# Moving the start of the FFN's moving operands from chunk to chunk

## The chip, the cores and the metric

The kernel runs on one core of a Trainium2 chip. The metric is the device time of one execution in microseconds. Before the change two runs took 2716.68 and 2721.58 us, median 2719.13 us.

## The reference

For each of 8 sequences of 3008 tokens and 256 features the reference takes a real FFT along the sequence, applies a complex linear layer (`w_r`, `w_i`, biases), shrinks real and imaginary parts towards zero by 0.01, and transforms back. All 24064 tokens then pass a feed-forward network (FFN) with 2048 hidden features:

```python
X = np.fft.rfft(x, axis=1)                      # per sequence
Yr = Xr @ w_r - Xi @ w_i + b_r; Yi = Xr @ w_i + Xi @ w_r + b_i
Yr, Yi = shrink(Yr, 0.01), shrink(Yi, 0.01)
y = np.fft.irfft(Yr + 1j * Yi, n=3008, axis=1)
h = y @ w_in; g = h - np.tanh(h); out = g @ w_out
```

## The kernel before, in words

The FFT is split into 47 and 64 points, 3008 being 47 times 64. Three parts follow each other per sequence and overlap across sequences.

**Forward** (lines 196 to 250) transforms 47 points at a time: three one-pass matmuls with a moving operand of 94 x 512 (lines 225 to 227), or, for the first sequence, one full fp32 matmul (line 219), which the chip carries out as two records. **Spectrum** does the 64-point step (line 277), the linear layer (line 297, moving operand 128 x 256), the shrinking and the first inverse step (lines 332 to 334).

**Chunk** is the FFN, in 52 chunks. A chunk has 5 pairs of rows of 94 tokens, so n = 470 columns; the last two chunks have 282. `time` makes the last inverse step (line 415) and writes the result as two fp32r parts, `yh` by ScalarE (line 419) and `yl` by VectorE (line 420). Such a pair of parts, high and low, is how the kernel keeps fp32 precision with one-pass matmuls: a product is low times high, high times low, and high times high. For each of 16 blocks `f` of 128 hidden features, `up` runs six matmuls with `yh` and `yl` moving (line 428), then tanh on ScalarE (line 431), `g` on VectorE (line 433), `gh` on ScalarE (line 435) and `gl` on VectorE (line 437). `down` runs six matmuls with `gh` and `gl` moving into two accumulators `o` (line 449). That is 192 FFN matmuls a chunk and 9984 in the kernel. `store` copies `o` out and sends it off.

The order of all work on each engine is fixed by the order in which the program issues it. The last loop issues, for each step `g`, `up` of block `g + 2`, then the Forward, Spectrum and `time` work planned for that step, then `down` of block `g`. Between the last matmul of `up(f)` and the first of `down(f)` stand therefore two `down` and two `up` of neighbouring blocks. The PSUM tile `h` has two buffers, `gh` and `gl` three each, `yh` and `yl` two each.

Where tiles lie: the pool `const` comes first in on-chip memory, and in it the four weight tiles `win_h`, `win_l`, `wout_h`, `wout_l`, whose 512-byte blocks begin at 128 modulo 512 bytes in each partition. Then comes `below`, a tile of 128 + 8 floats of which only the first column is read, then everything else. In the FFN the moving tiles have rows of `PITCH` = 512 floats (2048 bytes), though only 470 are used, so that all buffers of `yh`, `yl`, `gh` and `gl` begin at the same place modulo 512, which is 160. The moving operands of lines 225 to 227, 297 and 332 to 334 begin at 160 too.

Of the kernel before, what the change touches and what calls it, by code (L numbers as in the profile page):

```python
# [10 lines left out]
F32 = mybir.dt.float32  # L11
F32R = mybir.dt.float32r
# [54 lines left out]
def spectral_ffn(ctx, tc, x, w_r, w_i, b_r, b_i, w_in, w_out, f1, f2, i1, i2, out):  # L67
    nc = tc.nc
    P = 128
# [3 lines left out]
    CT = CP * 94  # L73
    NF = FF // P
    PITCH = 512
    PSUM = bass.MemoryType.PSUM

    const = ctx.enter_context(tc.tile_pool(name="const", bufs=1))
    load = ctx.enter_context(tc.tile_pool(name="load", bufs=2))
    work = ctx.enter_context(tc.tile_pool(name="work", bufs=2))  # L80
    cvt = ctx.enter_context(tc.tile_pool(name="cvt", bufs=2))
    ffn = ctx.enter_context(tc.tile_pool(name="ffn", bufs=3))
# [114 lines left out]
    class Forward:  # L197
        def __init__(self, b, ch):
            self.b, self.ch = b, ch
            self.x, self.ps = {}, {}  # L200
# [141 lines left out]
    class WholeSpectrum(Spectrum):  # L342
# [28 lines left out]
        def shrink(self):  # L371
            y = self.add(lambda jj, ri: self.tb[jj * 64:(jj + 1) * 64, :])
            up = self.temp("up", "th")
            nc.scalar.activation(out=up, in_=y, func=AF.Relu, bias=below[:, :1])
            mn = self.mn = work.tile([P, 2, D], F32, name="mn", tag="tmp", bufs=4)
            nc.vector.tensor_scalar(out=mn, in0=y, scalar1=LAM, scalar2=0.0, op0=ALU.add, op1=ALU.min)
            self.up = up
# [15 lines left out]
    class Chunk:  # L393
        def __init__(self, c):
            self.c, self.n = c, sizes[c] * 94
            self.pairs = [(p // NP, p % NP) for p in range(begin[c], begin[c] + sizes[c])]

        def load(self, lo=0, hi=96):
# [9 lines left out]
        def time(self, t):  # L408
            n = self.n
            if t == 0:  # L410
                self.yh = work.tile([P, 2, PITCH], F32R, name="yh", tag="yh")
                self.yl = work.tile([P, 2, PITCH], F32R, name="yl", tag="yl")
            ps = ps_f.tile([P, 512], F32, name="ps_i2", tag="f")
            for k, (_, p) in enumerate(self.pairs):
                nc.tensor.matmul(  # L415
                    ps[:, k * 94:(k + 1) * 94], self.zt[:, k, t * P:(t + 1) * P], i2t[:, p * 94:(p + 1) * 94],
                    start=True, stop=True,
                )
            nc.scalar.copy(out=self.yh[:, t, :n], in_=ps[:, :n])
            nc.vector.tensor_tensor(out=self.yl[:, t, :n], in0=ps[:, :n], in1=self.yh[:, t, :n].bitcast(F32), op=ALU.subtract)  # L420

        def up(self, f):
            n = self.n
            h = ps_h.tile([P, 512], F32, name="h", tag="h")
            k = 0
            for lhs, rhs in ((win_l, self.yh), (win_h, self.yh), (win_h, self.yl)):
                for t in range(2):
                    nc.tensor.matmul(h[:, :n], lhs[:, t, f * P:(f + 1) * P], rhs[:, t, :n], start=k == 0, stop=k == 5)  # L428
                    k += 1
            th = ffn.tile([P, CT], F32, name="th", tag="th")  # L430
            nc.scalar.activation(out=th[:, :n], in_=h[:, :n], func=AF.Tanh)  # L431
            g = ffn.tile([P, CT], F32, name="g", tag="g")
            nc.vector.tensor_tensor(out=g[:, :n], in0=h[:, :n], in1=th[:, :n], op=ALU.subtract)  # L433
            gh = ffn.tile([P, PITCH], F32R, name="gh", tag="g_h")
            nc.scalar.copy(out=gh[:, :n], in_=g[:, :n])  # L435
            gl = ffn.tile([P, PITCH], F32R, name="gl", tag="g_l")
            nc.vector.tensor_tensor(out=gl[:, :n], in0=g[:, :n], in1=gh[:, :n].bitcast(F32), op=ALU.subtract)  # L437
            return gh, gl

# [56 lines left out]
    with tc.manual_schedule(engines={E.PE, E.Activation, E.DVE, E.Pool, E.SP}):  # L496
# [6 lines left out]
        def keep_warm(n):  # L503
            for _ in range(n):
                nc.tensor.matmul(idle, warm[:, :P], warm, start=True, stop=True)

        keep_warm(8)
        below = const.tile([P, P + 8], F32, name="below")
        nc.vector.memset(below, -LAM)
        f1f = load_whole(f1, [P, P], "f1")  # L510
        first = [Forward(0, ch) for ch in range(NP // XC)]
# [128 lines left out]
    for g in range(-AHEAD, len(order)):  # L640
        if g + AHEAD < len(order):
            c, f = order[g + AHEAD]
# [4 lines left out]
        c, f = order[g]  # L647
# [33 lines left out]
```

## Time and profile before

| | |
|---|---|
| median of two runs | 2719.13 us (2716.68 to 2721.58) |
| profiled execution | 2722.2 us; span of its instructions 2720.4 us |
| mean granted TensorE clock | 0.993 |
| busy, TensorE matmul (PE) | 2685.2 us, 99% |
| busy, weight loads (PEld) | 2388.2 us, 88% |
| busy, VectorE (DVE) / ScalarE (ACT) / GpSimd (POOL) | 1741.2 / 1369.4 / 58.1 us |

Times in the views are microseconds, and the last number of a group is the mean of one instruction in nanoseconds. Matmuls are pipelined: a 128 x 470 matmul is on record for about 370 ns, but the next one starts long before it ends. What a matmul costs the kernel is the distance from its start to the next one's start. "Lnnn" is a line of the kernel; `o<-gh,wout_h` reads "writes `o`, reads `gh` and `wout_h`".

### The profile page before, as it was taken

How to read it: one execution, taken by the hardware profiler on the slowest of the kernel's cores; microseconds unless marked ns; L12 is line 12 of the kernel's file. 1: busy time of each engine (PE TensorE's matmuls, PEld its weight loads, DVE VectorE, ACT ScalarE, POOL GpSimd, SP SyncE). 2: the span in 40 equal slices, each digit the busy share in tenths (PEclk: the TensorE clock that was granted, in tenths of full speed). 3: DMA queues.
4: the chain of work that ended last, by engine and by line, in shares of the span. 5: the costliest groups of instructions: out<-in, count | busy, mean ns of one | idle time of the engine just before them, and what ended most of it. 6: DMA issues, size and time to landing. Idle time of an engine off the chain costs nothing.

```text
span 2720.4 us, 36889 instructions
## 1 busy us (share of the span) xinstructions
PE 2685.2 (99%) x14114; PEld 2388.2 (88%) x14114; DVE 1741.2 (64%) x3059; ACT 1369.4 (50%) x2571; POOL 58.1 (2%) x47
## 2 busy tenths in 40 slices
PE   8799999999999999999999999999999999999999
PEld 6578888999889998899988999899988999998989
DVE  5696776666656666566665666657675666655555
ACT  3564455444554445544455454644446444444445
POOL 2140000000000000000000000000000000000000
PEclk8899999999999999999999999999999999999999
DMA  6532114111141113211123110311104111100000
GB/s 207 153 100 66 57 50 127 38 53 36 31 119 45 42 36 92 75 49 41 36 58 101 38 50 29 111 56 49 49 22 123 45 42 40 35 22 22 20 19 17
DMA packets 105217, 163.52 MB, mean 60 GB/s; under 512 B 7440, under 2 KB 71056, under 8 KB 104944
## 3 DMA queue, kind: packets, MB, share of 16 engines
q1 hardware_dynamic: 105040, 161.16, 19.6%
q8 instruction: 111, 1.82, 0.3%
q14 instruction: 66, 0.54, 0.1%
HBM read 86.16 MB, written 74.97 MB: 59 GB/s over the span
## 4 chain that ended last, share of the span: by engine, by line
PE 92%; DVE 5%; ACT 1%; DMA 1%; issue 1%; POOL 0%; SPq 0%; DVEq 0%; ACTq 0%; POOLq 0%
PE o L449 36%; PE h L428 36%; PE ps_v L297 4%; PE ps_i L415 4%; PE ps_f L277 3%; PE ps_t L297 2%; PE ps_f L225 1%; DVE y L322 1%; PE ps_f L226 1%; PE ps_f L227 1%; PE ps_i L333 1%; PE ps_i L334 1%; PE ps_i L332 1%; DVE g L433 1%; DVE gl L437 0%
## 5 line engine op out<-in xcount | busy, mean ns | idle before, releaser
L433 DVE TENSOR_TENSOR g<-h,th 128x470 f32<-128x470 f32 (+1 forms) x832 | 531.5, 639 | 557.0 <-ACT th L431 549.3
L431 ACT ACTIVATE th<-h 128x470 f32<-128x470 f32 (+1 forms) x832 | 463.1, 557 | 769.8 <-PE h L428 769.4
L437 DVE TENSOR_TENSOR gl<-g,gh 128x470 fp32r<-128x470 f32 (+1 forms) x832 | 532.2, 640 | 288.9 <-ACT gh L435 205.0
L435 ACT CAST gh<-g 128x470 fp32r<-128x470 f32 (+1 forms) x832 | 483.0, 581 | 393.5 <-DVE g L433 385.5
L449 PE MATMUL o<-gh,wout_l 128*128 128x470 f32 (+1 forms) x1664 | 633.3, 381 | 0.8 <-ACT gh L435 0.8
L449 PE MATMUL o<-gl,wout_h 128*128 128x470 f32 (+1 forms) x1664 | 616.9, 371 | 2.6 <-DVE gl L437 2.6
L449 PE MATMUL o<-gh,wout_h 128*128 128x470 f32 (+1 forms) x1664 | 616.4, 370 | 0.0
L428 PE MATMUL h<-yh,win_l 128*128 128x470 f32 (+1 forms) x1664 | 482.4, 371 | 5.2 <-DVE g L433 4.7
L428 PE MATMUL h<-yl,win_h 128*128 128x470 f32 (+1 forms) x1664 | 481.2, 370 | 0.0
L428 PE MATMUL h<-yh,win_h 128*128 128x470 f32 (+1 forms) x1664 | 481.2, 370 | 0.0
L449 PEld LDWEIGHTS o<-gl,wout_h 128*128 128x128 f32 x1664 | 313.2, 188 | 44.4 <-DVE gl L437 5.7
L428 PEld LDWEIGHTS h<-yh,win_l 128*128 128x128 f32 x1664 | 310.5, 188 | 44.4 <-DVE g L433 6.6
L449 PEld LDWEIGHTS o<-gh,wout_l 128*128 128x128 f32 x1664 | 313.6, 188 | 36.5 <-issue 1.5
L428 PEld LDWEIGHTS h<-yl,win_h 128*128 128x128 f32 x1664 | 311.3, 188 | 35.7
L428 PEld LDWEIGHTS h<-yh,win_h 128*128 128x128 f32 x1664 | 311.2, 188 | 35.6
L449 PEld LDWEIGHTS o<-gh,wout_h 128*128 128x128 f32 x1664 | 314.0, 189 | 32.2
L322 DVE TENSOR_TENSOR y<-tb,ps_v 64x256 f32<-64x256 f32 x384 | 160.0, 417 | 13.1 <-ACT tb L369 9.1
L415 PEld LDWEIGHTS ps_i<-i,zin 96*128 96x128 f32 x1024 | 128.6, 195 | 5.4 <-issue 2.2
L415 PE MATMUL ps_i<-i,zin 96*128 96x94 f32 x1024 | 130.1, 275 | 1.4 <-DMA zin<-z 1.4
L277 PEld LDWEIGHTS ps_f<-f,at 128*128 128x128 f32 x768 | 101.2, 192 | 14.1 <-issue 9.0
L277 PE MATMUL ps_f<-f,at 128*128 128x128 f32 x768 | 102.8, 276 | 6.5 <-DMA at<-a 6.5
L92 DVE TENSOR_TENSOR x_l<-xt,x_h 94x512 fp32r<-94x512 f32 x112 | 78.6, 708 | 44.8 <-ACT x_h L91 44.8
(99 smaller groups left out, 2103.6 us busy)
## 6 DMA issues: line engine op xcount, KB each, us to landing
xt<-in_x SPq DMA_DIRECT2D x64, 384.0 KB, 3.7
at<-a SPq DMA_DIRECT2D x96, 256.0 KB, 2.8
z<-zo SPq DMA_DIRECT2D x96, 256.0 KB, 2.4
out<-ot SPq DMA_DIRECT2D x50, 470.0 KB, 3.0
a<-st SPq DMA_DIRECT2D x56, 384.0 KB, 3.1
zin<-z SPq DMA_DIRECT2D x42, 480.0 KB, 4.2
w_raw<-in_moe_w_in SPq DMA_DIRECT2D x8, 512.0 KB, 4.3
w_raw<-in_moe_w_out SPq DMA_DIRECT2D x8, 512.0 KB, 3.9
```

The source lines that it names most:

```text
L92: rest.tensor_tensor(out=lo, in0=src, in1=hi.bitcast(F32), op=ALU.subtract)
L225: nc.tensor.matmul(pv, f1h, xl, start=True, stop=False)
L277: nc.tensor.matmul(pv[:, t, jj], self.at[:, jj, t * P:(t + 1) * P], rhs, start=True, stop=True)
L297: nc.tensor.matmul(dst, lhs[:, t], rhs[:, t, :], start=n == 0, stop=n == 5)
L322: nc.vector.tensor_tensor(out=y[ri * 64:(ri + 1) * 64, jj, :], in0=common(jj, ri), in1=self.vv[jj * 64:(jj + 1) * 64, ri * D:(ri + 1) * D] ...
L415: nc.tensor.matmul(ps[:, k * 94:(k + 1) * 94], self.zt[:, k, t * P:(t + 1) * P], i2t[:, p * 94:(p + 1) * 94], start=True, stop=True,)
L428: nc.tensor.matmul(h[:, :n], lhs[:, t, f * P:(f + 1) * P], rhs[:, t, :n], start=k == 0, stop=k == 5)
L431: nc.scalar.activation(out=th[:, :n], in_=h[:, :n], func=AF.Tanh)
L433: nc.vector.tensor_tensor(out=g[:, :n], in0=h[:, :n], in1=th[:, :n], op=ALU.subtract)
L435: nc.scalar.copy(out=gh[:, :n], in_=g[:, :n])
L437: nc.vector.tensor_tensor(out=gl[:, :n], in0=g[:, :n], in1=gh[:, :n].bitcast(F32), op=ALU.subtract)
L449: nc.tensor.matmul(self.o[t][:, :n], lhs[:, f, t * P:(t + 1) * P], rhs[:, :n], start=f == 0 and k == 0, stop=f == NF - 1 and k == 2,)
```

## The change

Each chunk `c` gets a number `at` = 2 * (c % 21) floats, that is 0, 8, ..., 160 bytes, and its `yh`, `yl`, `gh` and `gl` begin that far into their tiles. `below` loses its 8 spare floats, so everything allocated after it lies 32 bytes lower: the tiles begin at 128 modulo 512, and the FFN's moving operands at 128 + 8 * (c % 21). The largest `at` is 40 floats, and 40 + 470 fits in the row of 512. The number, size and order of instructions stay as they were. The same starts are written by ScalarE (`yh`, `gh`) and VectorE (`yl`, `gl`).

```diff
     class Chunk:
         def __init__(self, c):
             self.c, self.n = c, sizes[c] * 94
+            self.at = 2 * (c % 21)
...
-                self.yh = work.tile([P, 2, PITCH], F32R, name="yh", tag="yh")
-                self.yl = work.tile([P, 2, PITCH], F32R, name="yl", tag="yl")
+                self.yh = work.tile([P, 2, PITCH], F32R, name="yh", tag="yh")[:, :, self.at:self.at + CT]
+                self.yl = work.tile([P, 2, PITCH], F32R, name="yl", tag="yl")[:, :, self.at:self.at + CT]
...
-            gh = ffn.tile([P, PITCH], F32R, name="gh", tag="g_h")
+            gh = ffn.tile([P, PITCH], F32R, name="gh", tag="g_h")[:, self.at:]
...
-            gl = ffn.tile([P, PITCH], F32R, name="gl", tag="g_l")
+            gl = ffn.tile([P, PITCH], F32R, name="gl", tag="g_l")[:, self.at:]
...
-        below = const.tile([P, P + 8], F32, name="below")
+        below = const.tile([P, P], F32, name="below")
```

## The prediction

> **What bounds the kernel now.** I read the page first: the busy shares, the granted clock in slices, and the chain of waits that ended last.
>
> ```profile
> PE 2685.2 (99%) x14114; PEld 2388.2 (88%) x14114; DVE 1741.2 (64%) x3059; ACT 1369.4 (50%) x2571; POOL 58.1 (2%) x47
> ...
> PE   8799999999999999999999999999999999999999
> ...
> PEclk8899999999999999999999999999999999999999
> ...
> PE 92%; DVE 5%; ACT 1%; DMA 1%; issue 1%; POOL 0%; SPq 0%; DVEq 0%; ACTq 0%; POOLq 0%
> PE o L449 36%; PE h L428 36%; PE ps_v L297 4%; PE ps_i L415 4%; PE ps_f L277 3%; PE ps_t L297 2%; PE ps_f L225 1%; DVE y L322 1%; PE ps_f L226 1%; PE ps_f L227 1%; PE ps_i L333 1%; PE ps_i L334 1%; PE ps_i L332 1%; DVE g L433 1%; DVE gl L437 0%
> ```
>
> TensorE is 92% of the chain, at nearly full clock after the first slices, and the two FFN lines are 72% of it. The busy times by stretch show that it hardly ever waits (columns: stretch, length, then busy us and instructions of PE, PEld, DVE, ACT, POOL, clock, DMA):
>
> ```profile
> 100.00:220.00 120.00, 105.61 (x438) 82.87 (x439) 91.55 (x149) 68.68 (x126) 29.56 (x20) 0.90 0.44 126
> ...
> 460.00:2366.00 1906.00, 1905.45 (x10170) 1714.89 (x10169) 1232.63 (x2167) 965.78 (x1814) 0.00 (x0) 1.00 0.18 55
> 2366.00:2660.00 294.00, 294.00 (x1463) 264.47 (x1462) 155.17 (x243) 137.40 (x243) 0.00 (x0) 1.00 0.06 21
> ```
>
> From 460 to 2660 us TensorE is idle for about half a microsecond. So the time is the number of matmuls times the distance between their starts, and a nanosecond on each FFN matmul is 9984 x 1 ns = 10 us. The distance stands in the timeline of the FFN-only stretch, twelve matmuls (one `up`, one `down`) apart, and again for the last chunks' narrow matmuls:
>
> ```profile
> 2501.27 0.58 PE L428 MATMUL h<-yh,win_l 128*128 128x470 f32 x2
> ...
> 2503.79 0.58 PE L428 MATMUL h<-yh,win_l 128*128 128x470 f32 x2
> ```
> ```profile
> 2697.51 0.42 PE L428 MATMUL h<-yh,win_l 128*128 128x282 f32 x2
> ...
> 2699.03 0.42 PE L428 MATMUL h<-yh,win_l 128*128 128x282 f32 x2
> ```
>
> 2.52 us / 12 = 0.2100 us for 470 columns, 1.52 / 12 = 0.1267 us for 282. The line through the two has 0.0833 / 188 = 0.443 ns a column and 0.002 us beside it. The whole FFN is 50 x 192 x 0.2100 + 2 x 192 x 0.1267 = 2016 + 49 = 2065 us, 76% of the span. (The chain says 72%, since in places it runs through DVE while PE was busy.)
>
> **The change part by part.** No instruction is added or removed. What moves is where operands begin.
>
> *The moving reads of lines 428 and 449.* They begin at 160 modulo 512 now and will begin at 128 + 8r, r = c % 21. Of the 52 chunks each r from 0 to 9 falls on three and each r from 10 to 20 on two. Three chunks (r = 4) keep 160; seven (r = 4, 12, 20) keep 160's place modulo 64; 15 begin at a multiple of 32 (every fourth r); 25 begin 8 past a multiple of 16 (odd r). The trace shows no one-pass matmul at another start than 160, so the price must be bounded from the nearest rows. Those are other one-pass matmuls, from the chain in a mixed stretch (start, us until the next piece):
>
> ```profile
> 387.74 1.46 PE ps_v L297 x12
> ...
> 390.05 0.24 PE ps_f L225
> 390.29 0.23 PE ps_f L226
> 390.52 0.23 PE ps_f L227
> 390.75 0.23 PE ps_i L332
> 390.98 0.23 PE ps_i L333
> 391.21 0.23 PE ps_i L334
> 391.43 0.23 PE ps_f L225
> ```
>
> Lines 332 to 334 take (391.43 - 390.75) / 3 = 0.227 us for 512 columns, where the line through the FFN's two points gives 0.229. Line 225 takes 0.24, by rounding at least 0.235, 3% over. Line 297 takes 1.46 / 12 = 0.122 us for 256 columns, where the line gives 0.1155: 5% over. All of them begin at 160, so these spreads come from something else than the start (which weights load meanwhile, how short the matmul is); they bound how far a one-pass stream here departs from the FFN's pace. The FFN is at the lower end, so there is more room above than below. Upwards: 3% of 2065 is 62 us and 5% is 103 us, if every chunk paid. [...] I take zero between +103 and -133. [...]
>
> [...]
>
> *The writes of `yh`, `gh` (ScalarE) and `yl`, `gl` (VectorE).* They take the same starts. Their present lengths and their cover:
>
> ```profile
> L437 DVE TENSOR_TENSOR gl<-g,gh 128x470 fp32r<-128x470 f32 (+1 forms) x832 | 532.2, 640 | 288.9 <-ACT gh L435 205.0
> L435 ACT CAST gh<-g 128x470 fp32r<-128x470 f32 (+1 forms) x832 | 483.0, 581 | 393.5 <-DVE g L433 385.5
> ```
> ```profile
> 2502.53 0.37 PE L449 MATMUL o<-gh,wout_l 128*128 128x470 f32 x1
> ...
> 2503.38 0.65 DVE L433 TENSOR_TENSOR g<-h,th 128x470 f32<-128x470 f32 x1 [0.57 <-ACT th L431]
> ...
> 2504.07 0.59 ACT L435 CAST gh<-g 128x470 fp32r<-128x470 f32 x1 [0.71 <-DVE g L433]
> ```
>
> `up(f)` ends its issue at 2502.53. `gh` is done at 2504.07 + 0.59 = 2504.66, `gl` 0.65 later at 2505.31. `down(f)` follows two `down` and two `up` later, 4 x 1.26 = 5.04 us, at 2507.57: 2.3 us to spare. A tenth more on each write (58 + 64 ns) is hidden nineteen times over, and so would a doubling be in this stretch. In the mixed stretch DVE is busy 1232.63 of 1906 us and ACT 965.78, so the cover is thinner there, but PE's half microsecond of idle says it has not run out. Price: zero, and below zero it cannot go, since nobody waits for these writes.
>
> *`below` shrinks by 32 bytes*, which moves all later tiles from 160 to 128: the moving operands of lines 225 to 227 (336 matmuls x 0.23 = 77 us), 297 (1512 x 0.122 = 184 us) and 332 to 334 (252 x 0.23 = 58 us). 319 us at the same 3% either way is +-10 us. I take zero. SP's DMAs keep their number and sizes and land in tiles 32 bytes lower; a chunk's load is issued six steps, 6 x 2.52 = 15 us, before its use.
>
> Sum: 2722.2 us of the profiled execution + 0 = 2722; the median of the two runs is 3 us under the profiled one, so 2720 on the scale of the runs.
>
> **The rivals.**
>
> *Some starts make the stream slower.* Mechanism: the read of the moving operand and the load of the next weights run at the same time (PEld is busy 88%), and the weights' 512-byte blocks begin at 128 modulo 512; now the moving run starts 32 bytes behind, and the change brings it to 0 to 160 bytes, and off the 32-byte grid in 37 chunks. For it: the 3% and 5% of lines 225 and 297 show that pace does vary. Against it: those vary at one and the same start. Priced at line 225's 3.5% (7.3 ns) the odd starts, 25 chunks, cost 25 x 192 x 7.3 ns = 35 us: 2755. All 37 off the grid cost 52 us: 2772. At line 297's 5% (10.5 ns) in 45 chunks, all but those at 160 modulo 64, 91 us: 2811. It decides from a mean of 5.4 ns. Chance 0.30, of which 0.21 beyond 2%.
>
> [...]
>
> *Some starts make it faster.* [...] Chance 0.10, half beyond 2%.
>
> [...]
>
> *The writes slow down enough to be seen.* A doubled `gl` adds 0.64 us per block; in the mixed stretch, about 37 chunks x 16 = 592 blocks, DVE would be busy 1233 + 379 of 1906 us. Were a sixth of it exposed, +63 us: 2785. Against it: 2.3 us of lead. Chance 0.04, 0.03 of it beyond 2%.
>
> *The starts do not matter at all, but the 32 bytes do*, for the other matmuls: 2710 to 2730, inside the forecast's own range. Chance 0.06.
>
> **How the numbers follow.** The forecast, no dependence, has 0.50, with 2710 to 2732 as its own range. Two per cent, about what a measurement can tell here, is 54 us. Slower: 0.21 + 0.03 = 0.24; faster 0.05; within 0.71. The range goes up to 2800, through the first rival's cases but the last, and down to 2690, a small share of fast starts. Left out are some 0.09 above and 0.07 below.
>
> **What would show it.** In the timeline of each chunk twelve matmuls would again stand 2.52 us apart, for every r alike, and the FFN groups keep their means. A dependence would show as stretches of one chunk's length with another distance, returning after 21 chunks; the first rival as more than 2.52 in odd chunks or off the grid, the second as less. `gh` or `gl` longer than 581 or 640 ns with PE still at 99% would show the writes slowed and hidden. The prediction is wrong if the mean distance moves by more than 5 ns.

## The result and the profile after

The changed kernel takes 2742.76 us (two runs, 2742.04 and 2743.47) against 2719.13: a ratio of 1.0084, 95% interval 1.0068 to 1.0101. It is slower by 0.84%, inside the 2% that the prediction counted as no change, and clearly outside the scatter of the runs. The profiled execution took 2742.0 us, its span is 2740.3.

The page of the changed kernel, its busy shares, its chain and the two groups that write `gl` and `gh` (line numbers are one higher in the functions that the diff touches):

```profile
PE 2705.6 (99%) x14114; PEld 2387.1 (87%) x14114; DVE 1742.5 (64%) x3059; ACT 1373.1 (50%) x2571; POOL 58.3 (2%) x47
...
PE 94%; DVE 4%; ACT 1%; issue 1%; DMA 0%; POOL 0%; DVEq 0%; ACTq 0%; SPq 0%; POOLq 0%
...
L438 DVE TENSOR_TENSOR gl<-g,gh 128x470 fp32r<-128x470 f32 (+1 forms) x832 | 532.0, 640 | 288.6 <-ACT gh L436 213.4
...
L436 ACT CAST gh<-g 128x470 fp32r<-128x470 f32 (+1 forms) x832 | 482.8, 580 | 390.7 <-DVE g L434 380.9
```

`gl` takes 640 ns as before and `gh` 580 against 581: at these starts the writes take what they took at 160. TensorE is still busy for 99% of the span, now 2705.6 us against 2685.2. The stretches show the same from the other side:

```profile
100.00:220.00 120.00, 107.16 (x458) 83.27 (x457) 92.45 (x151) 68.43 (x125) 29.67 (x20) 0.94 0.43 126
...
460.00:2366.00 1906.00, 1905.79 (x10079) 1699.98 (x10078) 1223.79 (x2153) 961.27 (x1801) 0.00 (x0) 1.00 0.18 55
2366.00:2660.00 294.00, 294.00 (x1444) 261.42 (x1443) 153.25 (x239) 135.53 (x239) 0.00 (x0) 1.00 0.07 24
```

From 460 to 2366 us TensorE gets 10079 matmuls done where it got 10170, with hardly any idle time in either and the clock at 1.00. So each matmul is further from the next. How far depends on the chunk. These are pairs of lines twelve matmuls apart (one `up` and one `down`), from the timeline of the changed kernel: chunk 46 (begins at 160, as before the change), chunk 48 (at 176) and chunk 36 (at 248).

```profile
2523.03 0.58 PE L429 MATMUL h<-yh,win_l 128*128 128x470 f32 x2
...
2525.55 0.37 PE L429 MATMUL h<-yh,win_l 128*128 128x470 f32 x1
...
2603.95 0.59 PE L429 MATMUL h<-yh,win_l 128*128 128x470 f32 x2
...
2606.51 0.38 PE L429 MATMUL h<-yh,win_l 128*128 128x470 f32 x1
...
2043.58 0.60 PE L429 MATMUL h<-yh,win_l 128*128 128x470 f32 x2
...
2046.22 0.38 PE L429 MATMUL h<-yh,win_l 128*128 128x470 f32 x1
```

2.52, 2.56 and 2.64 us for twelve: 210.0, 213.3 and 220.0 ns each. Over all chunks the mean distances from one start to the next are below. They are taken from the start times in the trace, from the third chunk on, between FFN matmuls of 470 columns that stand among FFN matmuls, without the few distances over 226 ns. The kernel before has 210.5 ns for all its chunks by the same reckoning.

| begins at (mod 512) | 128 | 136 | 144 | 152 | 160 | 168 | 176 | 184 | 192 | 200 | 208 |
|---|---|---|---|---|---|---|---|---|---|---|---|
| changed kernel, ns | 213.4 | 214.1 | 212.1 | 213.3 | **210.5** | 213.6 | 213.3 | 213.5 | 213.3 | 213.2 | 212.1 |

| begins at (mod 512) | 216 | 224 | 232 | 240 | 248 | 256 | 264 | 272 | 280 | 288 |
|---|---|---|---|---|---|---|---|---|---|---|
| changed kernel, ns | 213.2 | 214.4 | 213.5 | 211.6 | **219.1** | 213.3 | 212.6 | 216.4 | 214.3 | 214.0 |

Chunks with the same start, 21 apart, agree within 1.5 ns. Only 160 keeps the old distance; every other start costs more, 248 the most.

Some of these means hide more than one steady pace. Chunk 44 (at 144) takes 2.53 us for twelve matmuls over eight such spans, and 2.60 at its end, with all moving operands at the same start; between the two stand matmuls of line 416, the next chunk's `time`:

```profile
2446.98 0.58 PE L429 MATMUL h<-yh,win_l 128*128 128x470 f32 x2
...
2449.51 0.58 PE L429 MATMUL h<-yh,win_l 128*128 128x470 f32 x2
...
2450.78 1.25 PE L416 MATMUL ps_i<-i,zin 96*128 96x94 f32 x10
...
2456.96 1.25 PE L416 MATMUL ps_i<-i,zin 96*128 96x94 f32 x10
...
2459.38 0.59 PE L429 MATMUL h<-yh,win_l 128*128 128x470 f32 x2
...
2461.98 0.59 PE L429 MATMUL h<-yh,win_l 128*128 128x470 f32 x2
```

In chunk 43, at 136, the pace goes the other way at such a place, from 2.60 to 2.54 us. So at some starts the place alone does not fix the pace; what else picks it was not tested. At 160 and 248 the settled pace is the same in every chunk.

Weighted by the chunks, the 470-column matmuls lose 28.5 us and the two narrow chunks (131.1 and 130.0 ns where 127.0 stood) 1.4 us. The sums over the whole trace, from the third chunk's first matmul on, give 24.5 us: 14.9 on line 429 and 9.6 on line 450. Of the 5.4 us between these two accounts, 1.2 are the first two chunks, which the second account leaves out. Most of the rest are distances at which an FFN matmul stands beside other work: there are 1027 of them from the third chunk on, 236.9 us in sum before and 236.3 after, so they carry no price, where 3.0 ns each would have been 3 us. At the third chunk's first matmul the changed kernel is 4.3 us ahead, under a higher granted clock in the first 220 us (0.94 against 0.90 from 100 to 220 us). 24.5 - 4.3 = 20.2 us, and the spans differ by 19.9. From there on, the other one-pass matmuls (lines 225 to 227, 297, 332 to 334) changed by 0.1 us or less on each line.

### The profile page after: what moved, and what is told of

Read it like the earlier page. It is cut to its first block, busy times and chain, and to the rows that moved or that the text cites. A ratio compares the mean times of both kernels' runs of the same rounds, so it can differ in the third digit from the quotient of the medians.

```text
span 2740.3 us, 36889 instructions
## 1 busy us (share of the span) xinstructions
PE 2705.6 (99%) x14114; PEld 2387.1 (87%) x14114; DVE 1742.5 (64%) x3059; ACT 1373.1 (50%) x2571; POOL 58.3 (2%) x47
## 4 chain that ended last, share of the span: by engine, by line
PE 94%; DVE 4%; ACT 1%; issue 1%; DMA 0%; POOL 0%; DVEq 0%; ACTq 0%; SPq 0%; POOLq 0%
PE o L450 37%; PE h L429 37%; PE ps_v L297 4%; PE ps_i L416 4%; PE ps_f L277 3%; PE ps_t L297 2%; PE ps_f L225 1%; PE ps_f L227 1%; PE ps_f L226 1%; DVE y L322 1%; PE ps_i L333 1%; PE ps_i L332 1%; PE ps_i L334 1%; PE ps_f L219 1%; DVE gl L438 0%
## 5 line engine op out<-in xcount | busy, mean ns | idle before, releaser
L438 DVE TENSOR_TENSOR gl<-g,gh 128x470 fp32r<-128x470 f32 (+1 forms) x832 | 532.0, 640 | 288.6 <-ACT gh L436 213.4
```

## The experiments

Three theories of why the start matters. A: the place of the moving operand itself. B: its distance to the block of weights that TensorE loads at the same time (in the changed kernel weight loads are on record for 2387.1 us of the span, matmuls for 2705.6); these blocks begin at 128 modulo 512, so 160 is a distance of 32 bytes and 248 one of 120. C: its distance to the tiles that ScalarE and VectorE use meanwhile. e3_below_only, e8_cp4_272 and e12_both256 were run four, six and ten times; the others ran once, so their totals have no interval, and what they show rests on the distances between starts.

### e1_weights32: the weights moved, nothing else

```diff
+    const.tile([P, 8], F32, name="pad")
     win_h = const.tile([P, 2, FF], F32R, name="win_h")
...
-        below = const.tile([P, P], F32, name="below")
+        below = const.tile([P, P - 8], F32, name="below")
```

> The changed kernel with the four weight tiles 32 bytes later (160 modulo 512 instead of 128) and all else where it was; the moving operands still sweep 128 to 288. In the changed kernel the clean distances between matmul starts were lowest at 160 (210.5 ns) and highest at 248 (219.1 ns), about 213 ns at most others. Theory A, the moving operand's own place decides: 160 stays at 210.5 and 248 at 219. Theory B, the distance to the weight block that loads meanwhile decides: the curve moves by 32 bytes, so 192 falls to 210.5 (from 213.3), 160 rises to 213.4, 280 rises to 219 (from 214.3) and 248 falls to 213. The total stays near 2743 under both.

Measured 2740.43 us. The same kind of lines from this run's timeline, chunk 36 (at 248, now distance 88), chunk 40 (at 280, distance 120) and chunk 8 (at 192, distance 32):

```profile
2041.87 0.59 PE L430 MATMUL h<-yh,win_l 128*128 128x470 f32 x2
...
2044.43 0.38 PE L430 MATMUL h<-yh,win_l 128*128 128x470 f32 x1
...
2238.28 0.60 PE L430 MATMUL h<-yh,win_l 128*128 128x470 f32 x2
...
2240.92 0.38 PE L430 MATMUL h<-yh,win_l 128*128 128x470 f32 x1
...
575.74 0.58 PE L430 MATMUL h<-yh,win_l 128*128 128x470 f32 x2
...
578.26 0.37 PE L430 MATMUL h<-yh,win_l 128*128 128x470 f32 x1
```

248 has 2.56 us for twelve where it had 2.64, 280 has 2.64 and 192 has 2.52. The means: 192 fell from 213.3 to 210.6, 160 rose from 210.5 to 213.5, 280 rose from 214.3 to 219.4, 248 fell from 219.1 to 213.3. The whole curve moved by the 32 bytes of the weights: at the 17 starts that can be compared, the values agree within 1 ns. Theory A falls, and B holds in so far as the distance to the weights decides.

### e2_sweep160: the sweep without the part on `below`

```diff
-        below = const.tile([P, P], F32, name="below")
+        below = const.tile([P, P + 8], F32, name="below")
```

> The change without its part on below: weights at 128, every other tile back at 160, the moving operands sweep 160 to 320. Theories A and B alike: 160 (now chunks with c % 21 = 0) has 210.5 ns and 248 (c % 21 = 11) has 219 ns, as in the changed kernel. Theory C, the distance to the tiles that ScalarE and VectorE read and write meanwhile (th, g, which move back by 32 bytes too) decides: the low value is at 192 and the high one at 280. Total about 2740 to 2750; the starts from 296 to 320 are new, no value is expected of them.

Measured 2745.51 us. These lines are from a chunk at 160 and one at 248, again twelve matmuls apart:

```profile
2377.84 0.58 PE L429 MATMUL h<-yh,win_l 128*128 128x470 f32 x2
...
2380.36 0.37 PE L429 MATMUL h<-yh,win_l 128*128 128x470 f32 x1
...
734.27 0.60 PE L429 MATMUL h<-yh,win_l 128*128 128x470 f32 x2
...
736.91 0.38 PE L429 MATMUL h<-yh,win_l 128*128 128x470 f32 x1
```

2.52 and 2.64 us: 160 has a mean of 210.6 ns and 248 of 219.4, although `th`, `g` and all other tiles behind `below` lie 32 bytes elsewhere; 192 has 213.3. Theory C falls. The new starts 296 to 320 have 212.6, 212.3, 213.3 and 215.8.

### e3_below_only: the part on `below` alone

```diff
-        below = const.tile([P, P + 8], F32, name="below")
+        below = const.tile([P, P], F32, name="below")
```
(in the kernel before)

> The kernel before with the part on below alone: all moving operands fixed at 128 modulo 512, at distance 0 from the weight blocks. Theories A and B: every FFN matmul takes what the changed kernel's chunks at 128 take, 213.4 ns against 210.4, so 9600 x 3.0 + 384 x 3 ns = 30 us more than before: 2749. If the moved 32 bytes of the other matmuls matter, the total departs from that by up to 10 us while the FFN distance is still 213.4.

Measured 2745.36 us, ratio 1.0091 (1.0075 to 1.0108), and 213.4 ns per FFN matmul. The timeline has 2.56 us for twelve:

```profile
2523.48 0.59 PE L428 MATMUL h<-yh,win_l 128*128 128x470 f32 x2
...
2526.04 0.38 PE L428 MATMUL h<-yh,win_l 128*128 128x470 f32 x1
```

Taking 32 bytes off a tile of which one column is read costs as much as the whole change, because it puts every moving operand of the FFN at distance 0.

### e4_map: the whole of 512 bytes, with narrower chunks

```diff
-    CP = 5
+    CP = 4
...
-            self.at = 2 * (c % 21)
+            self.at = 2 * (c % 64)
```
(in the changed kernel)

> The change with chunks of 4 pairs (376 columns, 64 chunks) and a start that runs through all 64 multiples of 8 in 512 bytes, once each, from 128 up. It computes the same output in smaller chunks. The line through 282 and 470 columns gives 168.6 ns for 376 columns at the place of before. If the price of a start is paid once per matmul, 248 has about 177 ns and 160 about 169; if it goes with the columns, 248 has 175.5. If the curve repeats within 512 bytes (every 64 or 128), 160's low value comes back at 224, 288 and so on; the changed kernel shows that it does not at 224 and 288, so one low region within 512 is expected. Total 64 x 192 x 172 ns = 2114 us for the FFN against 2065 before, so about 2780 to 2820.

Measured 2762.27 us, under the 2780 to 2820 that were expected, and the one low region within 512 bytes did not come: the map, that is the distance between matmuls by place, repeats after 256 bytes. The starts 16 and 272 have 167.6 ns both, 208 and 464 have 167.7, 8 and 264 have 174.6; the two places of a pair differ by 1.6 ns at most. But it is another map than that of 470 columns. 160, the best place there, has 173.1 ns, and 248, the worst, 172.2; the cheapest are 272 and 208 (distances 144 and 80). So the price of a place is neither a fixed sum per matmul nor one per column, the two cases of the expectation; the best and the worst place change with the width.

### e5_win32: different weights at different places

```diff
+    const.tile([P, 8], F32, name="pad")
     win_h = const.tile([P, 2, FF], F32R, name="win_h")
...
+    const.tile([P, 120], F32, name="pad2")
     wout_h = const.tile([P, NF, D], F32R, name="wout_h")
...
-        below = const.tile([P, P], F32, name="below")
+        below = const.tile([P, 8], F32, name="below")
```
(in the changed kernel)

> Weights of the first FFN matrix (win) at 160, those of the second (wout) at 128, every later tile at 160, moving operands sweep 160 to 320. The distance to the weight blocks is then 0 to 160 bytes for line 428's matmuls and 32 to 192 for line 449's. Theory B: within a chunk the two lines take different times, each by its own distance. At 248: 213 ns for up (distance 88), 219 for down (120). At 280: 219 for up (120), 213 for down. At 160: 213.4 up, 210.5 down; at 192 the reverse. B1, the weights a matmul itself uses decide: the sixth matmul of up goes with the other five. B2, the weights that load meanwhile, for the next matmul, decide: the sixth of up goes with the down group, and the sixth of down with the up group.

Measured 2743.85 us. Within one chunk the two lines part, here by the first five matmuls of each group: at 248 `up` has 213.4 ns and `down` 217.8 (median 220), at 280 `up` has 215.8 and `down` 212.9, at 192 `up` has 210.8 and `down` 213.5. That is B, less sharp than in chunks where both are alike: `up` at distance 120 is below 219 and `down` at 32 (start 160) has 212.3, not 210.5. Perhaps a group of six is not long enough to settle; that was not tested. Whether a matmul's own weights (B1) or the next one's (B2) count stays open: the sixth of `up` has 215.7 at 248, 213.7 at 280 and 214.4 at 192, of which the last two fit B2 alone and the first neither; the sixth of `down` has 210.7, 214.1 and 212.9, which fits neither at 248, lies between the two at 280 and is nearer to B1 at 192.

### e6_all248: the worst place for all

```diff
-            self.at = 2 * (c % 21)
+            self.at = 30
```
(in the changed kernel)

> The change with one start, 248, in every chunk (distance 120 from the weight blocks). Theory B, and A as well: 219 ns for every 470-column matmul, 8.6 ns over before: 9600 x 8.6 = 83 us, some 5 us of it absorbed where matmuls wait anyway: 2795 to 2805, 3% slower than before. If the price depended on the mix of starts in neighbouring chunks it would be less.

Measured 2795.19 us, and 219.3 ns for 470 columns:

```profile
2568.16 0.60 PE L429 MATMUL h<-yh,win_l 128*128 128x470 f32 x2
...
2570.80 0.38 PE L429 MATMUL h<-yh,win_l 128*128 128x470 f32 x1
```

2.64 us for twelve. 8.8 ns x 9600 = 84 us, of which 76 show in the total. The narrow chunks have 131.8 ns, 4.7 over. The place of the FFN's moving operands alone is worth 2.8% here, by one run.

### e7_fine and e11_fine2: steps of 4 bytes

```diff
+    const.tile([P, 16], F32, name="pad")
     win_h = const.tile([P, 2, FF], F32R, name="win_h")
...
-            self.at = 2 * (c % 21)
+            self.at = c % 42
...
-        below = const.tile([P, P], F32, name="below")
+        below = const.tile([P, P - 16], F32, name="below")
```
(in the changed kernel, e7_fine; in e11_fine2 the pad has 120 floats, `below` 8, and the weights lie at 96)

> Weights at 192, all else at 128, moving operands in 42 steps of 4 bytes from 128 to 292: distances -64 to 100. Theory B with a period of 256 bytes (seen in the run with 376 columns): the multiples of 8 repeat the known curve, 210.5 ns at distance 32 (start 224), 213 to 214 at 0, 8, 24, 40, 48; distances 200 to 216 (starts 136 to 152) are new. If the read goes by 8-byte words, a start 4 past a multiple of 8 takes what its lower neighbour takes, within a nanosecond; if by single values, it has a value of its own. Total 2735 to 2750.

> Weights at 96, all else at 128, 470 columns, moving starts in 42 steps of 4 bytes from 128: distances 32 to 196, of which those from 104 up were tried only at multiples of 8. Theory B: the multiples of 8 repeat, 210.5 ns at 32 (start 128, 213.4 in the changed kernel), 219 at 120 (start 216), 213 at most. A value a step under 210, 206.7 ns, somewhere would be a better place for the kernel before, worth 32 us; I expect none. Total 2740 to 2755.

Measured 2747.48 and 2750.52 us. The multiples of 8 repeat: distance 32 has 210.5 and 210.6 ns at two more places (224 and 128), distance 120 has 219.1. A start 4 past a multiple of 8 has a value of its own: distances 28, 32 and 36 have 213.0, 210.5 and 213.3; 20, 52 and 60 have 216.7, 217.2 and 217.7. Two other distances are as good as 32, 108 (210.2) and 236 (210.5), and none is better by as much as 1 ns. That the period is 256 bytes at 470 columns too is tested at two places only: -64 and -60 have 215.1 and 216.2 ns in e7_fine, 192 and 196 have 215.9 and 216.5 in e11_fine2.

### e8_cp4_272 and e10_cp4_fine: narrow chunks at their best place

```diff
-    CP = 5
+    CP = 4
...
-            self.at = 2 * (c % 21)
+            self.at = 36
```
(in the changed kernel; e10_cp4_fine has `self.at = c % 64`)

> Chunks of 376 columns, all at 272 (distance 144), one of the two cheapest starts of the run with 64 starts: 167.6 ns where that run's mean was 172.1. Its 2762 us fall by 64 x 192 x 4.5 ns = 56 us to 2706, 0.5% under the kernel before. If the price hung on the mix of starts, it would stay nearer 2762. It computes the same output in 64 chunks of 4 pairs.

> Chunks of 376 columns, moving starts in 64 steps of 4 bytes from 128 to 380, distances 0 to 252, one whole period. The steady distances so far lie on steps of 3.33 ns (twelve matmuls take 2.52, 2.56, 2.60 or 2.64 us at 470 columns). The multiples of 8 repeat the earlier map: about 167 ns at 272 and 208, 171 to 174 at most others. Open: whether a start 4 past a multiple of 8 reaches the next step down, 163.3 ns, which would be worth 64 x 192 x 3.3 = 41 us. Of 51 starts tried at 4 bytes with 470 columns none reached a lower step than the best multiple of 8, so I expect none here: minimum 167 and a total near 2762.

e8_cp4_272 took 2710.97 us, ratio to the kernel before 0.9967 (0.9954 to 0.9979), and so beats both kernels, if by a third of a per cent; 2706 had been expected. Its timeline, twelve matmuls of 376 columns apart:

```profile
2500.31 0.50 PE L429 MATMUL h<-yh,win_l 128*128 128x376 f32 x2
...
2502.31 0.50 PE L429 MATMUL h<-yh,win_l 128*128 128x376 f32 x2
```

2.00 us / 12 = 166.7 ns, 0.443 ns a column against 0.447 at 470 columns. e10_cp4_fine took 2763.26 us: over the whole period of 256 bytes in steps of 4 nothing is under 167.6 ns, which distance 144 has. It meets the multiples of 8 among other neighbouring work than e4_map, and at 31 of the 32 it lies within 2 ns of a value there. At 248 bytes it has 173.3 ns where e4_map has 170.6 and 169.0: again one distance with more than one pace. (The expectation's count of 51 starts should read 42.)

### e9_probe: the load made shorter

```diff
         keep_warm(8)
+        NM = 470
+
+        def args(cols, at):
+            return idle[:cols, :NM], warm[:, :cols], warm[:, at:at + NM]
+
+        for _ in range(24):
+            nc.tensor.matmul(*args(128, 0), start=True, stop=True)
+        for _ in range(48):
+            nc.tensor.matmul(*args(128, 8), start=True, stop=True)
...
```
(in the kernel before; so on for 128, 64 and 32 columns, each at 8, 30 and 0 floats)

> The kernel before with some 456 extra matmuls of zeros behind its first warming ones: 470 columns from one tile, in groups of 48 with stationary blocks of 128, 64 and 32 columns, each at distances 32, 120 and 0 bytes from the weight block (which lies in the same tile). Their time adds some 100 us to the total, which is not the point. With 128 columns theory B expects the known 210.5, 219 and 213.4 ns also where both operands lie in one tile. [...]

Measured 2815.03 us with the extra matmuls. The timeline of the groups, in the order 128, 64, 32 stationary columns, each at distance 32, 120 and 0 bytes:

```profile
11.24 10.26 PE L516 MATMUL idle<-warm 128*128 128x470 f32 x48
21.33 10.71 PE L518 MATMUL idle<-warm 128*128 128x470 f32 x48
31.88 10.40 PE L520 MATMUL idle<-warm 128*128 128x470 f32 x48
42.12 10.27 PE L522 MATMUL idle<-warm 128*64 128x470 f32 x48
52.23 10.20 PE L524 MATMUL idle<-warm 128*64 128x470 f32 x48
62.26 10.41 PE L526 MATMUL idle<-warm 128*64 128x470 f32 x48
72.51 10.47 PE L528 MATMUL idle<-warm 128*32 128x470 f32 x48
82.81 10.39 PE L530 MATMUL idle<-warm 128*32 128x470 f32 x48
93.04 10.61 PE L532 MATMUL idle<-warm 128*32 128x470 f32 x48
```

From the start of one group to that of the next, divided by 48: 210.2, 219.8 and 213.3 ns with 128 columns. By the order of the program the other compute engines, but for the first memsets, wait meanwhile for line 219, which stands behind these groups (ScalarE's line 241 waits 110.5 us for it in this run), the data are zeros and both operands lie in one tile, and the three values are those of the FFN. With 64 columns they are 210.6, 209.0 and 213.5, and with 32 columns 214.6, 213.1 and (from the distances between starts) 217.6. The groups of weight loads themselves:

```profile
L516 PEld LDWEIGHTS idle<-warm 128*128 128x128 f32 x48 | 9.0, 188 | 1.1
...
L524 PEld LDWEIGHTS idle<-warm 128*64 128x64 f32 x48 | 6.4, 134 | 3.6
...
L530 PEld LDWEIGHTS idle<-warm 128*32 128x32 f32 x48 | 5.2, 108 | 5.0
```

A load of 32 columns takes 108 ns instead of 188, but the stream is no faster for it: 213.1 to 217.6 ns, where 128 columns have 210.2 to 219.8. The spread by place is 4.5 ns there and 9.6 with 128 columns. The bad distance of 128-column blocks, 120, is the best of the three for narrower ones (209.0 ns with 64 columns, 213.1 with 32). So the map depends on the number of stationary columns as on the width of the stream. That it is the shorter load which does it is not shown, since fewer stationary columns also mean fewer rows of output.

### e12_both256: a bad place and its cure

```diff
+    const.tile([P, 24], F32, name="pad")
     win_h = const.tile([P, 2, FF], F32R, name="win_h")
...
-            self.at = 2 * (c % 21)
+            self.at = 32
...
-        below = const.tile([P, P], F32, name="below")
+        below = const.tile([P, P - 24], F32, name="below")
```
(in the changed kernel)

> All moving operands of the FFN at 256, where the changed kernel took 213.3 ns, and the weight tiles moved by 96 bytes to 224, so that the distance is 32 as in the kernel before. Theory B: 210.5 ns and the time of before, 2719 us, within its 0.2%. Theory A: 213.3 ns, about 2745 as with all at 128.

Measured 2723.33 us, ratio to the kernel before 1.0009 (0.9999 to 1.0019), with 210.4 ns per matmul:

```profile
2523.36 0.58 PE L430 MATMUL h<-yh,win_l 128*128 128x470 f32 x2
...
2525.88 0.58 PE L430 MATMUL h<-yh,win_l 128*128 128x470 f32 x2
```

2.52 us for twelve at 256, where the changed kernel took 2.56. With the distance back at 32 bytes the time of before is back, at a place that had cost 3 ns. This and e1_weights32 are what shows that the distance to the weights is the cause.

## Why the prediction was right and wrong

**The bound was read rightly.** The kernel is the number of matmuls times the distance between their starts, and the change came out as that: 24.5 us more on lines 429 and 450, and next to nothing on the other matmuls. "A nanosecond on each FFN matmul is 9984 x 1 ns = 10 us" held nearly: e6_all248's 8.8 ns made 76 us.

**The step that failed is "I take zero between +103 and -133".** The mean start costs 3.0 ns per 470-column matmul, 28.5 us by the clean distances. The upper bound came from the spreads of lines 225 and 297, which "come from something else than the start" since all began at 160. They begin at one place, but their weights do not (`f1_l` and `f1_h` lie at different places, the weights of line 297 are the data), and e1_weights32 shows that the distance to the weights counts: with the weights alone moved, 160 rose from 210.5 to 213.5 ns. The rows that bounded the price may well have been the effect itself; no run moved those operands one by one. No run shows the term of -133, which would be some 13 ns less on each of the 9984 FFN matmuls, nor the small share of fast starts at the lower end of the range: of all starts tried at 470 columns the best mean is 210.2 ns, against 210.5 before. The text saw "more room above than below" and still put the likeliest value at zero. Nor is the price of a bad start one sum per matmul: at 248 it was 8.8 ns at 470 columns and 4.7 at 282 (e6_all248).

**The first rival came true in what it measured by, and not in size.** It named the weights' load beside the moving read as the cause and the distance from 128 as the measure. e1_weights32 and e12_both256 show the measure. That it is the load running beside the matmul which costs the time was the author's argument and is not shown: e5_win32 left open whose weights count. Its price list was wrong: not the odd starts, nor those off the 32-byte grid, but every start except 160 pays, most of them some 3 ns, 248 nearly 9. Its sum of 35 to 91 us met 24.5. It was given 0.30, with 0.21 for more than 2%; the mean of 3.0 ns stayed under the 5.4 ns (54 us over 9984 matmuls) from which it would have decided.

**The second rival fell.** No start of this change, nor any of the finer ones, is faster than 160 by as much as 1 ns in the mean: the lowest is 210.2 ns, at distance 108, against 210.5, among all 64 four-byte places of a period (e7_fine and e11_fine2 together).

**The writes** cost nothing: 580 and 640 ns, as said. **The 32 bytes of `below`** cost the other matmuls nothing, as said, and they did matter for the FFN: e3_below_only shows 2745 us from them alone, a case that the prediction did not price because it looked at the starts only together.

**The range and the chances.** 2743 lies inside 2690 to 2800, and within 2%, which had 0.71. But 0.50 of that stood on a case with no dependence, with 2710 to 2732 as its own range, and that case was false: the answer fell into the class by luck, through a dependence whose mean is 0.84%. Of the signs named ahead, the one for no dependence, 2.52 us for every start alike, did not come. The one for a dependence did: stretches of one chunk's length with another distance, returning after 21 chunks.

## What to carry to other kernels

Here TensorE was busy for 1905.8 of 1906 us, so that the distance between matmul starts was the time, and it depended on addresses that no line of the kernel states: on the distance, modulo 256 bytes, between the moving operand and the blocks of weights (210.5 ns at 32 bytes, 219.1 at 120). Give such operands rows of equal pitch so that the distance is the same everywhere, and measure a few distances; the best one changed with the width of the matmul (32 bytes at 470 columns, 144 at 376), so it must be sought again when the tile width changes. An edit of a small tile early in the allocation moves everything behind it; in e3_below_only that alone cost 0.9% (2745.36 us, ratio 1.0091), so an unexplained change of that size is worth a look at the start-to-start distances.

## What the runs showed of the hardware that was not expected

- Twelve settled matmuls of 470 columns mostly take 2.52, 2.56, 2.60 or 2.64 us: steps of 0.04 / 12 us = 3.33 ns per matmul. 166.7 and 173.3 ns at 376 columns and 126.7 at 282 lie on the same grid. It is not a rule, since chunk 44 of the changed kernel held 2.53 us over eight spans.
- At some distances more than one pace is steady, and a few other matmuls in between can switch it: 2.53 and 2.60 us in chunk 44, 2.60 and 2.54 in chunk 43.
- The map repeats after 256 bytes (the starts 16 and 272 both have 167.6 ns at 376 columns) and is sharp: distances of 28, 32 and 36 bytes have 213.0, 210.5 and 213.3 ns.
- It depends on the width of the stream (best distance 32 at 470 columns, 144 at 376) and on the number of stationary columns (distance 120 takes 219.8 ns with 128 of them and 209.0 with 64).
- With 128 stationary columns, zeros from one tile, while the other compute engines wait for line 219 (ScalarE 110.5 us), take what the FFN takes at the three distances tried: 213.3, 210.2 and 219.8 ns at 0, 32 and 120. So there neither the data nor the other engines' work make the difference.
